# A causal convolution and two MLPs on one core: the startup re-ordered, and the low halves of two chunks made by one subtraction

## The chip, the cores and the metric

The kernel runs on one core of a Trainium2 chip. Its time is the device time of one execution in microseconds, from the first to the last instruction with what lies around it. Three runs of the kernel before took 2321.36, 2321.87 and 2329.53 us; the median is 2321.87 us. The profile comes from a further execution.

## The reference

The input is 4 sequences of 4096 positions with 192 channels. A causal convolution of width 7 (softmax weights, one set per group of 24 channels) is followed by two MLPs of width 2048 on the 16384 positions. The weights of the MLPs arrive in float64.

```python
x_pad = np.concatenate([np.zeros((B, pad, D), dtype=np.float32), x], axis=1)
out = np.einsum('hk,bskhg->bshg', w, x_unf)          # w = softmax(weight), 7 taps
x = out.reshape(B * S, D)
h = x @ w_in;  x = (h - np.tanh(h)) @ w_out          # first MLP
h = np.maximum(x @ moe2_w_in, 0.0);  out = h * h @ moe2_w_out   # second MLP
```

## The kernel before

The positions are cut into 32 blocks of 512. Activations are held with channels on partitions, and each fp32 operand of an MLP product is held as a high and a low part (`h` and `l` at the end of a tile's name); a product is three matmuls, high by high, low by high and high by low. A **unit** (m, b, p) is MLP m, block b and a pair p of two chunks of 128 hidden features, so a block has 8 units in each MLP and the program has 512. The contraction is split into row halves of 64 partitions, so that one matmul of each half can run beside the other on the array.

One step of the main loop (line 554 on) issues, for unit u, the 18 half-height matmuls of its first product (`ph`), and the second product (`pA`, `pB`) of the units two and three steps back. Both are laid into 19 slots of two matmuls. Each chunk of the unit then passes through `act` (line 401) and `split` (line 414). For the first MLP, ScalarE (ACT) makes the tanh, VectorE (DVE) subtracts it from `ph` in place (line 406), ACT casts the high part `gh` (line 417), and DVE subtracts it to give the low part `gl` (line 419). The first chunk of a unit is split at the end of its step. The second is split in the middle of the next step.

All other work is put between these by hand. `side` is a list of operations for each half step, filled by `spread` (line 480): the weights' decoding from float64 bits (`decode_ops`, lines 124 to 160: one ACT operation and four DVE operations on `da`, then casts and subtractions into `wIh`, `wIl`, `wO`), the convolution of later blocks (`tap`, lines 230 and 233), the split of its result into `z` (lines 297 to 303) and the ends of blocks. Every engine takes its instructions in the order in which they are issued. Blocks 0 and 1 run side by side, so that each decoded pair of weights serves two units; `SKEW` (line 454) is how many units of block 0 come ahead of the first of block 1, and with it stand the steps in which the pairs are due (`due`, line 492).

The prologue (line 495) loads, computes the taps, and makes the convolution of blocks 0 and 1. For the channels 128 to 191 of both blocks (`xTb`) and for block 1 (`xTa`), TensorE does it with seven matmuls each against diagonal matrices that ACT writes into a `y` buffer (lines 248 and 254). For block 0's first 128 channels DVE does seven taps. The first pair of weights is decoded in the prologue; the others are spread over the steps.

Of the kernel before, what the change touches and what calls it, by code (L numbers as in the profile page):

```python
# [10 lines left out]
F32 = mybir.dt.float32  # L11
F32R = mybir.dt.float32r
# [3 lines left out]
ALU = mybir.AluOpType  # L16
# [14 lines left out]
def conv_mlp_mlp_kernel(ctx: ExitStack, tc: tile.TileContext, x, weight, w_in1, w_out1, w_in2, w_out2, out):  # L31
# [34 lines left out]
    cv = ctx.enter_context(tc.tile_pool(name="cv", bufs=2))  # L66
    zp = ctx.enter_context(tc.tile_pool(name="zp", bufs=2))
    yp = ctx.enter_context(tc.tile_pool(name="yp", bufs=3))
    work = ctx.enter_context(tc.tile_pool(name="work", bufs=3))
    op = ctx.enter_context(tc.tile_pool(name="op", bufs=1))  # L70
    ps_h = ctx.enter_context(tc.tile_pool(name="ps_h", bufs=4, space=PSUM))
    ps_a = ctx.enter_context(tc.tile_pool(name="ps_a", bufs=2, space=PSUM))
# [17 lines left out]
    def load_w(m, p, parts="io"):  # L90
        if (m, p) not in staged:
            staged[m, p] = dec.tile([P, CW], I64, name="st")
        st = staged[m, p]
        c = 2 * p * P
        if "i" in parts:
            load_in(m, st, c)
        if "o" in parts:
            nc.sync.dma_start(
                out=st[:, CI:].rearrange("p (u d) -> p u d", u=2),
                in_=w_out[m][c : c + 2 * P, :].rearrange("(u p) d -> p u d", u=2),  # L100
            )
# [108 lines left out]

    def load_a(b, q=None):
        if b == 1:
            t = work.tile([P, T], F32, name="t").rearrange("p (a c) -> p a c", c=32)
        else:
            t = cv.tile([P, TH, 32], F32, name="xa", bufs=1)
        xs["A", b] = t
        for j in range(4):
            (q or nc.sync).dma_start(out=t[32 * j : 32 * j + 32], in_=x_of(b)[j])
# [6 lines left out]
    def tap(p, b, k):  # L225
        i = "AB".index(p)
        t, w = xT[p, b], taps[:, i, k : k + 1]
        if k == 0:
            acc[p, b] = cv.tile([P, T], F32, name=f"acc{p}", bufs=1)
            nc.vector.tensor_scalar(acc[p, b], t[:, 0:T], w, None, op0=ALU.mult)  # L230
        else:
            a = acc[p, b]
            nc.vector.scalar_tensor_tensor(a, t[:, k : k + T], w, a, op0=ALU.mult, op1=ALU.add)
# [6 lines left out]

    diag = {}

    def make_diag(p):
        t = diag.setdefault("all", yp.tile([P, 4 * T], F32, name="y") if p == "B" else None)
        for k in range(K):
            n = k + K * (p == "A")
            d = diag[p, k] = t[:, n * P : (n + 1) * P]
            nc.scalar.mul(d, ident, taps[:, "AB".index(p), k : k + 1])

    def pe_conv(p, b):  # L250

        a = acc[p, b] = ps_h.tile([P, T], F32, name="ph")
        for k in range(K):
            nc.tensor.matmul(a, diag[p, k], xT[p, b][:, k : k + T], start=k == 0, stop=k == K - 1)  # L254

    def halo(dst, b, src):
        if b % BPB == 0:
# [80 lines left out]
    def products_2(m, b, p, i):  # L338

        if (m, b) not in acc_t:  # L340
            acc_t[m, b] = [ps_a.tile([P, T], F32, name=n) for n in ("pA", "pB")]
        pA, pB = acc_t[m, b]
        r = slice(0, P) if i is None else half(i)
        to_a, to_b = [], []
        for c in range(2):
            gh, gl = (t[r] for t in g_t[m, b, 2 * p + c])
            w = W[m]["O"][r, p, c]
            to_a += [(pA, w[:, 0:P], gh), (pA, w[:, D + DB :], gh), (pA, w[:, 0:P], gl)]
            to_b += [(pB, w[:, P : D + DB], gh), (pB, w[:, P : D + DB], gl)]
        first, last = p == 0 and i != 1, p == NP - 1 and i != 0  # L350
        flags = lambda ms: [(*q, first and k == 0, last and k == len(ms) - 1) for k, q in enumerate(ms)]
        return flags(to_a) + flags(to_b)
# [47 lines left out]

    def act(m, b, f):
        ph = h_t[m, b, f // 2][f % 2]
        t = t_t[m, b, f] = work.tile([P, T], F32, name="t")
        if m == 0:
            nc.scalar.activation(t, ph, AF.Tanh)  # L405
            nc.vector.tensor_tensor(t, ph, t, op=ALU.subtract)  # L406
        else:
            nc.scalar.activation(t, ph, AF.Relu)  # L408
            if b == 1 and f % 2:
                nc.vector.tensor_tensor(t, t, ph, op=ALU.mult)  # L410
            else:
                nc.scalar.activation(t, t, AF.Square)  # L412

    def split(m, b, f):
        t = t_t.pop((m, b, f))
        gh = work.tile([P, T], F32R, name="gh", bufs=6)
        nc.scalar.copy(gh, t)  # L417
        gl = work.tile([P, T], F32R, name="gl", bufs=6)
        nc.vector.tensor_tensor(gl, t, gh.bitcast(F32), op=ALU.subtract)  # L419
        g_t[m, b, f] = gh, gl  # L420

    def finish_ops(m, b):
        pA, pB = acc_t.pop((m, b))
# [27 lines left out]
        ]  # L451


    SKEW = 4

    def two_blocks(m):

# [37 lines left out]
    def prologue():  # L495
        nc.sync.dma_start(out=wt, in_=weight)
        load_b(0)
        load_a(0)
        load_w(0, 0, "i")
        load_a(1)  # L500
        load_w(0, 0, "o")
        load_w(0, 1)
        warm = wpool.tile([P, 1], F32, name="warm")
        nc.gpsimd.memset(warm, 0.0)
        nc.scalar.activation(warm, warm, AF.Tanh)
        make_identity(nc, ident)
        warm_pe(9)
        make_taps()
        head_b(0)
        warm_pe(7)  # L510
        w0 = decode_ops(0, 0, parts=((0, CI), (CI, CW)))
        z0 = split_ops(0)
        make_diag("B")
        pe_conv("B", 0)
        head_a(0)
        make_diag("A")
        tap("A", 0, 0)
        tap("A", 0, 1)
        tap("A", 0, 2)
        head_a(1)  # L520
        pe_conv("A", 1)
        w0[0]()
        for o in w0[1:4]:
            o()
        w0[4]()
        for k in range(3, K):
            tap("A", 0, k)
        w0[6]()
        z0[0]()
        w0[5]()  # L530
        z0[1]()
        z0[2]()
        for o in w0[7:]:
            o()


    after = {}
    spread(split_ops(1), 1, 4)
    for n in range(1, len(pairs)):
        ops = decode_ops(*pairs[n])  # L540
        if n + 1 < len(pairs):
            ops.insert(1, lambda n=n: load_w(*pairs[n + 1]))
        d = 2 * due[n]
        spread(ops, *((d - 2, d) if n < SKEW else (d - 5, d - 1)))
    side[2 * SKEW] += [lambda: load_a(2), lambda: load_b(2)]
    for b in range(2, NBLK):
        s = 2 * at[0, b, 0]
# [65 lines left out]
```

## Time and profile before

| | us |
|---|---|
| median of three runs | 2321.87 |
| profiled execution | 2329.7 |
| its span, first to last instruction | 2327.9 |
| PE, ACT, DVE busy in the span | 2309.2, 1619.3, 1467.7 |

The profiled execution took 2329.7 us, of which 1.8 lie outside the span. The page divides the span into 40 slices of 58 us and gives each engine's busy share in tenths. The first three slices are the prologue and the steps in which weights are decoded; from then on the rows hardly change. The parts that matter are read from views of single stretches: groups of instructions by shape, the instructions of one engine in order of time with what ended each idle time, and the busy time of each engine in a stretch.

### The profile page before, as it was taken

To read this page: it belongs to the slowest core of one execution; us is meant where nothing else is said; L and a number is where in the kernel's file an instruction comes from. 1 tells how busy PE (TensorE), PEld (TensorE's weight loads), DVE (VectorE), ACT (ScalarE), POOL (GpSimd) and SP (SyncE) were. 2 spreads that over 40 slices of the span, in tenths; PEclk is the share of its full clock that TensorE was granted. 3 is DMA by queue.
4 is the path that set the end of the run, shared out by engine and by line. 5 is a ranking of instruction groups with operands and counts; after the bars stand their busy time and mean duration, and the time that the engine had idled before them with its cause. 6 is when DMAs were issued, how large, how long until landed. Compare 5 with 4: busy or idle time off the path is not lost.

```text
span 2327.9 us, 50435 instructions
## 1 busy us (share of the span) xinstructions
PE 2309.2 (99%) x19500; PEld 1892.5 (81%) x19500; DVE 1467.7 (63%) x2299; ACT 1619.3 (70%) x2866; POOL 1.4 (0%) x15
## 2 busy tenths in 40 slices
PE   9999999999999999999999999999999999999999
PEld 6767888888888888888988888888888888888887
DVE  8986666656666555666557665566665666665553
ACT  5577766777666777667777667776677776677766
POOL 0000000000000000000000000000000000000000
PEclk8999999999999999999999999999999999999999
DMA  5230101101111101111001011010111011110000
GB/s 127 68 83 17 26 13 26 22 14 23 22 17 22 26 10 22 17 22 26 15 17 26 13 26 22 11 26 13 26 22 20 16 22 17 22 22 11 16 13 15
DMA packets 216864, 57.78 MB, mean 25 GB/s; under 512 B 204336, under 2 KB 210480, under 8 KB 216624
## 3 DMA queue, kind: packets, MB, share of 16 engines
q1 hardware_dynamic: 216624, 54.56, 11.6%
q8 instruction: 154, 2.52, 0.5%
q14 instruction: 86, 0.70, 0.1%
HBM read 25.17 MB, written 12.58 MB: 16 GB/s over the span
## 4 chain that ended last, share of the span: by engine, by line
PE 95%; DVE 2%; ACT 1%; issue 1%; DMA 0%; SPq 0%; POOL 0%; DVEq 0%; ACTq 0%; POOLq 0%
PE ph L359 38%; PE pA L359 33%; PE pB L359 22%; PE ph L254 1%; DVE t L406 0%; DVE da L138 0%; ACT gh L417 0%; DVE da L134 0%; PE ph L239 0%; DVE gl L419 0%; ACT t L405 0%; ACT da L124 0%; DVE da L129 0%; DVE wIl L155 0%; ACT t L408 0%
## 5 line engine op out<-in xcount | busy, mean ns | idle before, releaser
L359 PE MATMUL pA<-gh,wO 64*128 64x512 f32 x4088 | 1279.3, 392 | 0.0
L419 DVE TENSOR_TENSOR gl<-t,gh 128x512 fp32r<-128x512 f32 x1024 | 683.4, 688 | 623.2 <-ACT gh L417 589.9
L359 PE MATMUL ph<-z,wIh 64*128 64x512 f32 x3072 | 1011.0, 394 | 9.8 <-DVE t L406 7.4
L359 PE MATMUL ph<-y,wIh 64*128 64x512 f32 x3072 | 1003.2, 391 | 1.9 <-DVE t L410 1.9
L359 PEld LDWEIGHTS pA<-gh,wO 64*128 64x128 f32 x4088 | 753.9, 185 | 86.3 <-ACT gh L417 0.8
L359 PE MATMUL pB<-gl,wO 64*128 64x512 f32 x2044 | 804.4, 394 | 0.0
L359 PE MATMUL pB<-gh,wO 64*128 64x512 f32 x2044 | 801.7, 392 | 0.0
L359 PE MATMUL pA<-gl,wO 64*128 64x512 f32 x2044 | 800.8, 392 | 0.0
L417 ACT CAST gh<-t 128x512 fp32r<-128x512 f32 x1024 | 604.7, 613 | 99.1 <-DVE t L406 94.8
L359 PEld LDWEIGHTS ph<-z,wIh 64*128 64x128 f32 x3072 | 569.0, 185 | 75.3 <-DVE t L406 10.6
L359 PEld LDWEIGHTS ph<-y,wIh 64*128 64x128 f32 x3072 | 566.2, 184 | 60.5 <-DVE t L410 2.7
L359 PE MATMUL ph<-z,wIl 64*128 64x512 f32 x1536 | 604.7, 394 | 0.4 <-DVE wIl L155 0.3
L359 PE MATMUL ph<-y,wIl 64*128 64x512 f32 x1536 | 601.4, 392 | 0.0
L405 ACT ACTIVATE t<-ph 128x512 f32<-128x512 f32 x512 | 305.7, 598 | 364.2 <-PE ph L359 265.0
L406 DVE TENSOR_TENSOR t<-ph,t 128x512 f32<-128x512 f32 x512 | 351.9, 687 | 204.6 <-ACT t L405 203.7
L359 PEld LDWEIGHTS pA<-gl,wO 64*128 64x128 f32 x2044 | 376.8, 184 | 49.3 <-DVE gl L419 0.4
L359 PEld LDWEIGHTS pB<-gh,wO 64*128 64x128 f32 x2044 | 376.8, 184 | 48.0
L359 PEld LDWEIGHTS pB<-gl,wO 64*128 64x128 f32 x2044 | 376.4, 184 | 46.1
L408 ACT ACTIVATE t<-ph 128x512 f32<-128x512 f32 x512 | 305.1, 596 | 153.3 <-PE ph L359 130.4
L412 ACT ACTIVATE t<-t 128x512 f32<-128x512 f32 x504 | 318.8, 633 | 16.0
L359 PEld LDWEIGHTS ph<-z,wIl 64*128 64x128 f32 x1536 | 284.6, 185 | 28.4 <-DVE wIl L155 1.5
L359 PEld LDWEIGHTS ph<-y,wIl 64*128 64x128 f32 x1536 | 282.8, 184 | 27.5
(71 smaller groups left out, 712.0 us busy)
## 6 DMA issues: line engine op xcount, KB each, us to landing
z<-z SPq DMA_DIRECT2D x32, 256.0 KB
y<-y SPq DMA_DIRECT2D x32, 256.0 KB
out<-ua SPq DMA_DIRECT2D x128, 64.0 KB
xa<-in_x SPq DMA_DIRECT2D x124, 64.0 KB
st<-in_moe_w_out SPq DMA_DIRECT2D x16, 384.0 KB
xb<-in_x SPq DMA_DIRECT2D x64, 64.0 KB
st<-in_moe_w_in SPq DMA_DIRECT2D x16, 256.0 KB
out<-tu SPq DMA_DIRECT2D x64, 64.0 KB
```

The costliest lines, as they stand in the source:

```text
L254: nc.tensor.matmul(a, diag[p, k], xT[p, b][:, k : k + T], start=k == 0, stop=k == K - 1)
L359: ins = nc.tensor.matmul(o, w, r, start=start, stop=stop).ins
L405: nc.scalar.activation(t, ph, AF.Tanh)
L406: nc.vector.tensor_tensor(t, ph, t, op=ALU.subtract)
L408: nc.scalar.activation(t, ph, AF.Relu)
L412: nc.scalar.activation(t, t, AF.Square)
L417: nc.scalar.copy(gh, t)
L419: nc.vector.tensor_tensor(gl, t, gh.bitcast(F32), op=ALU.subtract)
```

## The change

There are five edits.

1. `split` makes `gh` and `gl` as tiles of two chunks. Each chunk's cast is made where it was, but the low part of both chunks is made by one subtraction over 1024 columns, behind the cast of the second chunk.
2. The convolution of block 0's first 128 channels is divided: DVE does taps 0 to 4, TensorE taps 5 and 6 into a `pA` bank, and DVE adds the two. ACT makes the diagonals for taps 0 to 4 later.
3. TensorE's convolution of block 1 is issued behind step 0, and the split of its result moves from steps 0 and 1 to steps 1 and 2. The results lie in `pA` and `pB` banks.
4. The second pair of weights is loaded ahead of block 1's input and decoded in the prologue.
5. `SKEW` is 3 instead of 4, which moves the due steps of pairs 3 to 7 back by one. The pool `work` holds two tiles of two chunks of `t` instead of three of one.

```diff
-    def make_diag(p):
+    def make_diag(p, ks=range(K)):
...
-        a = acc[p, b] = ps_h.tile([P, T], F32, name="ph")
-        for k in range(K):
-            nc.tensor.matmul(a, diag[p, k], xT[p, b][:, k : k + T], start=k == 0, stop=k == K - 1)
+        a = ps_a.tile([P, T], F32, name="p" + p)
+        for k in range(first, K):
+            nc.tensor.matmul(a, diag[p, k], xT[p, b][:, k : k + T], start=k == first, stop=k == K - 1)
+        if first:
+            nc.vector.tensor_tensor(acc[p, b], a, acc[p, b], op=ALU.add)
+        else:
+            acc[p, b] = a
...
     def split(m, b, f):
-        t = t_t.pop((m, b, f))
-        gh = work.tile([P, T], F32R, name="gh", bufs=6)
-        nc.scalar.copy(gh, t)
-        gl = work.tile([P, T], F32R, name="gl", bufs=6)
-        nc.vector.tensor_tensor(gl, t, gh.bitcast(F32), op=ALU.subtract)
-        g_t[m, b, f] = gh, gl
+
+        p = f // 2
+        if f % 2 == 0:
+            g_t[m, b, p] = [work.tile([P, 2, T], F32R, name=n, bufs=3) for n in ("gh", "gl")]
+        gh, gl = g_t[m, b, p]
+        nc.scalar.copy(gh[:, f % 2], t_t[m, b, p][:, f % 2])
+        if f % 2:
+            nc.vector.tensor_tensor(gl, t_t.pop((m, b, p)), gh.bitcast(F32), op=ALU.subtract)
...
-    SKEW = 4
+    SKEW = 3
...
         make_diag("B")
         pe_conv("B", 0)
         head_a(0)
-        make_diag("A")
-        tap("A", 0, 0)
-        tap("A", 0, 1)
-        tap("A", 0, 2)
-        head_a(1)
-        pe_conv("A", 1)
-        w0[0]()
-        for o in w0[1:4]:
+        make_diag("A", range(own, K))
+        for k in range(own):
+            tap("A", 0, k)
+        for o in w0[0:5]:
             o()
-        w0[4]()
-        for k in range(3, K):
-            tap("A", 0, k)
+        make_diag("A", range(own))
         w0[6]()
+        w0[5]()
+        for o in w0[7:10]:
+            o()
+        pe_conv("A", 0, own)
         z0[0]()
-        w0[5]()
         z0[1]()
         z0[2]()
-        for o in w0[7:]:
+        for o in w0[10:]:
             o()
...
-    after = {}
-    spread(split_ops(1), 1, 4)
-    for n in range(1, len(pairs)):
+        head_a(1)
+        w1[0]()
+        for o in w1[1:]:
+            o()
...
+    after = {0: [lambda: pe_conv("A", 1)]}
+    spread(split_ops(1), 3, 6)
+    side[0].append(lambda: load_w(0, 2))
+    for n in range(2, len(pairs)):
```

The first place is DVE where the second chunk of a unit ends, here with the decoding of a pair beside it. `t` is a chunk's activation, `gl` its low part, `da` and `wIl` are a pair of weights under decoding. Before:

```order
L406 TENSOR_TENSOR t<-ph,t 128x512
L419 TENSOR_TENSOR gl<-t,gh 128x512 x2
L134 SCALAR_TENSOR_TENSOR da<-st,da 128x768
L138 SCALAR_TENSOR_TENSOR da<-st,da 128x768
L406 TENSOR_TENSOR t<-ph,t 128x512
L155 TENSOR_TENSOR wIl_83<-da,wIh_82 128x384
```

And now, at the same place:

```order
L414 TENSOR_TENSOR t<-ph,t 128x512
L430 TENSOR_TENSOR gl<-t,gh 128x1024
L134 SCALAR_TENSOR_TENSOR da<-st,da 128x768
L138 SCALAR_TENSOR_TENSOR da<-st,da 128x768
L414 TENSOR_TENSOR t<-ph,t 128x512
L155 TENSOR_TENSOR wIl_83<-da,wIh_82 128x384
```

The two subtractions of one chunk each, of which the first belonged to the chunk that was finished earlier, have become one of both; nothing stands between it and the subtraction that finishes the second chunk.

The second place is the start of TensorE's program: `xTb` and `xTa` are the convolution's inputs, `y` the diagonals. Before, the two convolutions stand ahead of step 0 (its matmuls write `ph`):

```order
L254 MATMUL ph<-xTb,y 128x512 x7
L254 MATMUL ph<-xTa,y 128x512 x7
L359 MATMUL ph<-z,wIh_82 128x512
L359 MATMUL ph<-z,wIl_83 128x512
L359 MATMUL ph<-z,wIh_82 128x512 x2
```

And now (the middle of step 0 is left out):

```order
L256 MATMUL pB<-xTb,y 128x512 x7
L256 MATMUL pA<-xTa,y 128x512 x2
L365 MATMUL ph<-z,wIh_82 128x512
...
L365 MATMUL ph<-z,wIh_82 128x512
L256 MATMUL pA<-xTa,y 128x512 x7
L365 MATMUL ph<-z,wIh_82 128x512
```

Two matmuls for block 0 stand where seven for block 1 stood, and those seven stand between step 0 and step 1.

The third place is ACT's program in the prologue. Line 248 (now 250) writes the diagonals, line 124 begins the decoding of the first pair's input half and then of its output half, line 150 casts. Before:

```order
L248 ACTIVATE y<-ua,taps 128x128 x14
L260 COPY xTa<-xTa 128x6
L124 ACTIVATE da<-st 128x384
L150 CAST wIh_82<-da 128x384
L124 ACTIVATE da<-st 128x384
L297 CAST z<-ph 64x512
```

And now:

```order
L250 ACTIVATE y<-ua,taps 128x128 x9
L124 ACTIVATE da<-st 128x384
L150 CAST wIh_82<-da 128x384
L250 ACTIVATE y<-ua,taps 128x128 x5
L124 ACTIVATE da<-st 128x384
L303 CAST z<-pB 64x512
```

Five of the fourteen diagonals have moved behind the cast of the first weights and ahead of the operation with which the output half's decoding begins.

## Rows read from the trace of the kernel before

**Rows 1.** The page: busy time, DVE's busy tenths by slice.

```profile
PE 2309.2 (99%) x19500; PEld 1892.5 (81%) x19500; DVE 1467.7 (63%) x2299; ACT 1619.3 (70%) x2866; POOL 1.4 (0%) x15
...
DVE  8986666656666555666557665566665666665553
```

**Rows 2.** Busy time by stretch: length, engines (instructions), granted clock, DMA share, GB/s.

```profile
22.00:155.00 133.00, 122.86 (x913) 94.97 (x914) 124.60 (x208) 79.92 (x147) 0.00 (x0) 0.94 0.35 90
155.00:200.00 45.00, 43.14 (x364) 33.65 (x362) 33.56 (x56) 38.26 (x70) 0.00 (x0) 1.00 0.15 42
200.00:2250.00 2050.00, 2050.00 (x17575) 1691.22 (x17575) 1268.65 (x1962) 1435.87 (x2529) 0.60 (x6) 1.00 0.10 20
```

**Rows 3.** ACT in order of time: start, duration; first activations of units 0 and 24.

```profile
25.02 0.60 ACT L405 ACTIVATE t<-ph 128x512 f32<-128x512 f32 x1 [1.67 <-PE ph L359]
...
153.12 0.59 ACT L408 ACTIVATE t<-ph 128x512 f32<-128x512 f32 x1
```

**Rows 4.** Waits of PE, 22 to 200 us: total, times, longest.

```profile
PE ph L359 <- DVE t L406: 7.4, 9, 1.7
```

**Rows 5.** DVE in order of time, the end of one unit and the next's start.

```profile
54.12 0.69 DVE L406 TENSOR_TENSOR t<-ph,t 128x512 f32<-128x512 f32 x1
54.72 1.47 DVE L419 TENSOR_TENSOR gl<-t,gh 128x512 fp32r<-128x512 f32 x2
56.10 0.95 DVE L134 SCALAR_TENSOR_TENSOR da<-st,da 128x768 uint32<-128x768 uint32 x1
57.09 0.96 DVE L138 SCALAR_TENSOR_TENSOR da<-st,da 128x768 uint32<-128x768 uint32 x1
57.96 0.68 DVE L406 TENSOR_TENSOR t<-ph,t 128x512 f32<-128x512 f32 x1
```

**Rows 6.** ACT in the same stretch: the cast of the second chunk.

```profile
54.84 0.62 ACT L417 CAST gh<-t 128x512 fp32r<-128x512 f32 x1 [0.87 <-DVE t L406]
```

**Rows 7.** DVE's groups by shape: busy us, mean ns, idle before.

```profile
L419 DVE TENSOR_TENSOR gl<-t,gh 128x512 fp32r<-128x512 f32 x1024 | 683.4, 688 | 623.2 <-ACT gh L417 589.9 <-PE pB L359 10.6
...
L434 DVE TENSOR_TENSOR y<-pA,y 128x512 fp32r<-128x512 f32 x32 | 21.8, 681 | 0.0
...
L138 DVE SCALAR_TENSOR_TENSOR da<-st,da 128x768 uint32<-128x768 uint32 x15 | 14.4, 958 | 0.5
...
L155 DVE TENSOR_TENSOR wIl<-da,wIh 128x384 fp32r<-128x384 f32 x16 | 8.9, 554 | 1.9 <-ACT wIh L150 1.9
L130 DVE TENSOR_SCALAR da<-da 128x768 uint32<-128x768 uint32 x15 | 8.4, 560 | 0.5
```

**Rows 8.** DVE in the prologue, in order of time.

```profile
12.92 0.71 DVE L265 STREAM_TRANSPOSE xTa<-t 128x512 f32<-128x512 f32 x1 [2.69 <-DMA t<-in_x]
13.56 0.32 DVE L129 TENSOR_SCALAR da<-da 128x384 f32<-128x384 f32 x1
...
14.90 0.56 DVE L138 SCALAR_TENSOR_TENSOR da<-st,da 128x384 uint32<-128x384 uint32 x1
15.37 3.11 DVE L233 SCALAR_TENSOR_TENSOR accA<-xTa,taps,accA 128x512 f32<-128x512 f32 x4
```

**Rows 9.** ACT in the prologue: the diagonals, the start of the decoding.

```profile
7.72 4.20 ACT L248 ACTIVATE y<-ua,taps 128x128 f32<-128x128 f32 x14
...
11.92 0.55 ACT L124 ACTIVATE da<-st 128x384 f32<-128x384 f32 x1
15.49 0.51 ACT L150 CAST wIh<-da 128x384 fp32r<-128x384 f32 x1 [3.02 <-DVE da L138]
```

**Rows 10.** PE in the prologue: block 1's convolution, step 0's first matmul.

```profile
16.17 6.17 PE L254 MATMUL ph<-xTa,y 128*128 128x512 f32 x14
...
22.27 0.49 PE L359 MATMUL ph<-z,wIh 64*128 64x512 f32 x1
```

**Rows 11.** Busy time by stretch, cut where the granted clock changes; columns as in Rows 2.

```profile
10.70:27.76 17.06, 16.16 (x46) 7.93 (x45) 13.51 (x25) 7.95 (x19) 0.00 (x0) 1.00 0.49 136
27.76:41.41 13.65, 12.82 (x38) 9.31 (x39) 13.09 (x23) 6.31 (x11) 0.00 (x0) 0.50 0.49 137
```

More of the change, by code (lines that the diff above doesn't have):

```diff
@@ L68, in conv_mlp_mlp_kernel @@
     yp = ctx.enter_context(tc.tile_pool(name="yp", bufs=3))
-    work = ctx.enter_context(tc.tile_pool(name="work", bufs=3))
+    work = ctx.enter_context(tc.tile_pool(name="work", bufs=2))
     op = ctx.enter_context(tc.tile_pool(name="op", bufs=1))
@@ L212, in load_a @@
         if b == 1:
-            t = work.tile([P, T], F32, name="t").rearrange("p (a c) -> p a c", c=32)
+            t = work.tile([P, 2, T], F32, name="t")[:, 0, :].rearrange("p (a c) -> p a c", c=32)
         else:
@@ L241, in conv_mlp_mlp_kernel @@
     diag = {}
-    def make_diag(p):
-        t = diag.setdefault("all", yp.tile([P, 4 * T], F32, name="y") if p == "B" else None)
-        for k in range(K):
+    def make_diag(p, ks=range(K)):
+        if not diag:
+            diag["all"] = yp.tile([P, 4 * T], F32, name="y")
+        t = diag["all"]
+        for k in ks:
             n = k + K * (p == "A")
@@ L248, in make_diag, with pe_conv @@
             nc.scalar.mul(d, ident, taps[:, "AB".index(p), k : k + 1])
-    def pe_conv(p, b):
-        a = acc[p, b] = ps_h.tile([P, T], F32, name="ph")
-        for k in range(K):
-            nc.tensor.matmul(a, diag[p, k], xT[p, b][:, k : k + T], start=k == 0, stop=k == K - 1)
+    def pe_conv(p, b, first=0):
+        a = ps_a.tile([P, T], F32, name="p" + p)
[5 more added lines that the diff above has]
+            acc[p, b] = a
     def halo(dst, b, src):
@@ L345, in products_2 @@
         for c in range(2):
-            gh, gl = (t[r] for t in g_t[m, b, 2 * p + c])
+            gh, gl = (t[r, c] for t in g_t[m, b, p])
             w = W[m]["O"][r, p, c]
@@ L402, in act @@
         ph = h_t[m, b, f // 2][f % 2]
-        t = t_t[m, b, f] = work.tile([P, T], F32, name="t")
+        if f % 2 == 0:
+            t_t[m, b, f // 2] = work.tile([P, 2, T], F32, name="t")
+        t = t_t[m, b, f // 2][:, f % 2]
         if m == 0:
@@ L414, in split @@
     def split(m, b, f):
[L415 to L420 removed]
+        p = f // 2
+        if f % 2 == 0:
+            g_t[m, b, p] = [work.tile([P, 2, T], F32R, name=n, bufs=3) for n in ("gh", "gl")]
[3 more added lines that the diff above has]
+            nc.vector.tensor_tensor(gl, t_t.pop((m, b, p)), gh.bitcast(F32), op=ALU.subtract)
     def finish_ops(m, b):
@@ L498, in prologue @@
         load_a(0)
-        load_w(0, 0, "i")
+        load_w(0, 0)
+        load_w(0, 1)
         load_a(1)
-        load_w(0, 0, "o")
-        load_w(0, 1)
         warm = wpool.tile([P, 1], F32, name="warm")
@@ L511, in prologue @@
         w0 = decode_ops(0, 0, parts=((0, CI), (CI, CW)))
+        w1 = decode_ops(0, 1)
         z0 = split_ops(0)
+        own = 5
         make_diag("B")
@@ L543, in conv_mlp_mlp_kernel @@
         d = 2 * due[n]
-        spread(ops, *((d - 2, d) if n < SKEW else (d - 5, d - 1)))
+        spread(ops, *((1, 4) if n == 2 else (d - 5, d - 1)))
     side[2 * SKEW] += [lambda: load_a(2), lambda: load_b(2)]
```

## The prediction

> **What bounds the kernel now.** I read the page first, then busy time by stretch, then single engines in order of time where the rows change. On the page PE is busy 99% and DVE only 63%, but DVE's tenths begin with 8986 and settle at 5 or 6 [rows 1]. The stretches say why: from 22 to 155 us DVE is busy 124.60 of 133 us (94%) while PE makes 913 matmuls; from 200 to 2250 us DVE is at 62%, PE at 100% with 17575 matmuls in 2050 us [rows 2]. So there are two kernels in one. Most of it is paced by PE: 38 matmuls a unit give 2050 / (17575 / 38) = 4.43 us a unit. The first 24 units, all of the first MLP, are paced by DVE: their activations start at 25.02 and the 25th unit's at 153.12, which is 128.1 / 24 = 5.34 us a unit [rows 3]. That costs 24 x (5.34 - 4.43) = 21.8 us. PE waits there for the subtraction on line 406 [rows 4], which gives back a `ph` bank. Behind that stretch PE never waits, so what is lost or won there stays to the end, and what changes in the other 488 units hides behind PE.
>
> The change touches the 22 us before the first unit and the 128 us of the first 24. In both, DVE's queue is the place to count. A time in DVE's queue moves the end by the same amount, less what falls into the waits that it already has: 133 - 124.60 = 8.4 us, much of it the short gaps between dependent instructions [rows 2].
>
> **One subtraction for two chunks.** Before, DVE's order at the end of a unit is: the subtraction that finishes the second chunk at 54.12, the low part of the first chunk at 54.72 (it needs nothing new), the low part of the second, and the next work at 56.10 [rows 5]. Between, ACT casts the second chunk: it starts at 54.84, when the subtraction has ended, and ends at 55.46 [rows 6]. So the first chunk's low part lies exactly in the time that ACT needs, and DVE hardly stands still: 56.10 - 54.12 = 1.98 us a unit.
>
> After, the row behind the second chunk's subtraction is the merged one, and that needs the second cast. DVE takes its instructions in order, so it stands from 54.81 until 55.50 (0.69 us), and everything behind it (decoding, taps, the next unit's subtraction, for which PE waits) stands with it. Then comes a two-source subtraction of 1024 columns. No row has that shape. From below it costs more than 0.96 us, the 768-column row; from above not more than two of 0.69, 1.38 us [rows 7]. Between the 384-column row (0.554) and the 768-column row (0.958) a column costs 1.05 ns beside a fixed 0.15 us, so I take 0.958 + 256 x 1.05 ns = 1.23 us. The next instruction starts about 0.09 us before the end (57.09 + 0.96 against 57.96 [rows 5]), so it takes 1.14 us of the queue. A unit's end then takes 54.12 to 55.50 and 1.14: 2.52 us, 0.54 more than before. Over the 24 units that DVE paces: 24 x 0.54 = **+13.0 us**. With 0.96 (0.87 of the queue) a unit loses 0.27 and the sum is +6.5; with 1.38 (1.29) it loses 0.69 and the sum is +16.6.
>
> The Trainium skill, on the page VectorE: DVE Perf Modes, section "The TRN2 errata — SBUF-src ops pay a fixed extra latency per instruction", says that an instruction pays its fixed latency once however large the tile, so that one large tile is cheaper than two small ones. The rows agree that there is a fixed part (0.15 us of 0.69). By that rule alone the merge saves; it says nothing of a wait ahead of the instruction, and by itself it is the last rival below.
>
> In the other 232 units of the first MLP the same wait lies in DVE's idle time (38% of it [rows 2]), and in the second MLP the cast needs no DVE result except for the odd chunks of block 1. The low part comes later by half a step, but is read two steps on. I cost both at nothing; if that cover failed, PE would wait in each step, and 0.1 us each would be 49 us.
>
> **The prologue.** Four things happen to DVE's queue.
> - The wait of 2.69 us for block 1's input goes [rows 8], since its transpose is put behind the first pair's decoding, some 8 us later. -2.7.
> - Two taps go (four take 3.11, so 1.55) and one addition from PSUM comes, 0.68 like the subtraction from `pA` [rows 7]. -0.9.
> - ACT has nine diagonals instead of fourteen before the first decoding, and five of 0.30 us [rows 9] before the second. The five taps end at about 10.2 (12.92 - 2.69 [rows 8]) + 1.55 = 11.8, the input half is decoded 1.9 us later (13.56 to 15.46 [rows 8]), at 13.7; ACT casts until 14.2, writes five diagonals until 15.7 and makes the output half's first operation (0.55) until 16.2. DVE has one subtraction of 0.55 in that time and stands for 1.45. +1.45. About 0.5 more goes into short waits for casts that had a chunk's subtraction beside them before; this is an estimate.
> - Step 0 needs `z`, which follows the addition: about 19.7 instead of 22.27 [rows 10]. Its 18 half-height matmuls stand one behind the other, 0.233 us each (two at once take 2 x 2050 / 17575 [rows 2]), and end near 24.1. Block 1's convolution then takes its 6.2 us [rows 10], to 30.3, and step 1's first chunk is ready 12 matmuls and an activation later, at 33.7 or so. DVE's own queue, counted on from 16.2: output half 1.9 (18.1), addition and two subtractions for `z` with a cast between (20.3), `wO` and the transpose (21.5), the second pair's four instructions at 0.56 and 0.96 (24.6, [rows 7]) and its three subtractions with a wait for a cast (26.2), unit 0 with its stall and the four instructions of the third pair (3.1 + 0.6 + 2.5): 32.5. It waits for about 1.5.
>
> The sum is -2.7 - 0.9 + 1.45 + 0.5 + 1.5 = -0.2, call it nothing. The 2.6 us that step 0 starts earlier are not a gain by themselves, because PE isn't what is late: the convolution has moved from ahead of step 0 to behind it, and DVE's queue sets the pace.
>
> **Skew and loads.** The same pairs, taps and splits lie ahead of unit 24 before and after, in another order; with the queue full the order moves nothing. The split of block 1 comes later by a step, its copy to the other half too, and step 3 instead of step 4 waits for it; DVE stands at 40 us then and PE is not ahead. The load of pair 2 is issued at about 20 us and needed at 26. I cost these at nothing. The tail isn't touched: the last low part is needed by the last twelve matmuls alone.
>
> **Sum.** 2329.7 + 13.0 - 0.2 = 2342.5 against the profiled execution, which lies 7.8 above the median. The difference put on the median: 2321.87 + 12.8 = **2334.7 us**.
>
> **The rivals.**
> - *The clock falls in the prologue.* From 27.76 to 41.41 the granted clock was 0.50, its lower level of 1.2 GHz, after a stretch of half-height matmuls with a gap [rows 11]. Now PE ends taps 5 and 6 near 18 and idles until 19.7, then runs half-height matmuls until 24. If the clock falls there, the rest of step 0 (14 matmuls) takes 3.3 us more and about half of block 1's convolution another 3.1; step 1 comes up to 6.4 later and DVE, with an empty queue at 32.5, waits for it. With 5 of it: 2339.7. The Trainium skill, TensorE: Matmul & The Clock Gate, "The HAM clock gate", says that activity releases the throttle; the rows agree in that the clock came back. Against it: the convolution is full-height work and may bring the clock back early.
> - *The stall is mostly covered.* If the merged row costs as little as the 768-column row (+6.5) and some 2.5 of the 8.4 us in which DVE is not busy now take up the rest: +4, 2326. For it: ACT chains that DVE waits for may have come in by then. Against it: DVE's gaps in units like that of rows 5 are under 0.1 us.
> - *The merge saves* (the other side). If the merged subtraction is not held up, because it finds the cast done, a unit's end takes 1.98 - 1.38 + 1.14 = 1.74, that is 0.24 less: 24 x 0.24 = 5.8. With the 3.6 of the first two prologue items and no new waits there: -9.4, 2312.5; with the 2.6 us of step 0's earlier start on top, -12, 2310. It decides only where something of at least 0.6 us lies between the second chunk's subtraction and the merged one. Nothing does in the order.
>
> **How the numbers follow.** The forecast has 0.52 and its own range 2328 to 2339 (6.5 to 16.6 us). The clock has 0.20, the covered stall 0.18, the saving 0.10. The range 2317 to 2345 leaves out the better part of the saving and the worst of the clock (the runs before already differ by 8). A difference under 0.5%, 11.6 us, can't be told from none. Slower by more (over 2333.5): 0.65 of the forecast and all of the clock, 0.34 + 0.20 = 0.54. Faster by more (under 2310.3): 0.06, half of the saving's share and a little. Within: 0.40.
>
> **What would show it.** In the profile after, each of the first 24 merged subtractions should have an idle time of about 0.7 us before it, released by the cast, and last 1.2; a unit with decoding should take 0.5 more, and the 25th unit should start at about 166 instead of 153. DVE should have no wait for block 1's input, one of 1.5 for line 124's second half, and one for step 1's first activation. From 200 us on a unit should take 4.43 as before. It is wrong if the 25th unit starts before 160, if the merged rows show no wait, or if the steady units change.

## The result and the profile after

Four runs of each kernel on one chip: the changed kernel took 2343.78 to 2352.81 us, median 2352.42, the kernel before 2321.36 to 2330.15, median 2325.7. The ratio is 1.0106, 95% interval [1.0084, 1.0128]: it is slower, by some 25 us. The forecast was +12.8 and 2334.7, and 2352.4 lies above its range. The executions of one kernel spread over some 9 us, those of the kernel before in three groups near 2321, 2326.5 and 2330 us, so that medians of a few runs mix them; the parts are therefore told apart below by when a unit's first activation starts in the profiled execution, early enough that the groups haven't parted yet.

| first activation of unit (us) | 1 | 4 | 24 | 40 | 511 |
|---|---|---|---|---|---|
| before | 32.18 | 51.60 | 153.12 | 226.17 | 2314.27 |
| after | 39.85 | 59.01 | 170.55 | 249.19 | 2336.78 |
| later by | 7.67 | 7.41 | 17.43 | 23.02 | 22.51 |

So 7.4 us are lost by unit 4, another 10 by unit 24, 5.6 between units 24 and 40, and nothing after that. The page of the changed kernel has PE as busy as before; DVE has 513 instructions less and is idle more:

```profile
PE 2314.3 (98%) x19504; PEld 2032.2 (86%) x19504; DVE 1418.1 (60%) x1786; ACT 1623.0 (69%) x2866; POOL 1.4 (0%) x15
...
L365 PE MATMUL pA<-gh,wO 64*128 64x512 f32 x4088 | 1281.1, 393 | 9.9 <-DVE y L444 9.9
L430 DVE TENSOR_TENSOR gl<-t,gh 128x1024 fp32r<-128x1024 f32 x512 | 627.4, 1225 | 801.3 <-ACT gh L428 682.7
```

The last number of the `pA` row is new: PE has waited 9.9 us for DVE's line 444. The same three stretches as in [rows 2], for the changed kernel (length, busy time and instructions by engine, granted clock, DMA share, GB/s):

```profile
22.00:155.00 133.00, 115.73 (x793) 84.37 (x794) 107.76 (x164) 69.43 (x128) 0.00 (x0) 0.92 0.32 83
155.00:200.00 45.00, 37.81 (x304) 29.04 (x302) 34.36 (x49) 30.99 (x57) 0.00 (x0) 0.97 0.26 68
200.00:2250.00 2050.00, 2050.00 (x17575) 1830.45 (x17575) 1224.06 (x1503) 1443.70 (x2538) 0.61 (x6) 1.00 0.10 19
```

In the first stretch DVE's busy time fell from 124.60 to 107.76 and PE's matmuls from 913 to 793. DVE isn't fuller, it stands more; this is where a busy share misleads. From 155 to 200 PE made 304 matmuls where it made 364. From 200 on the 17575 matmuls are the same to the last one.

The merged subtraction looks as forecast. DVE in order of time, at the place of [rows 5], and ACT's cast there:

```profile
57.08 0.69 DVE L414 TENSOR_TENSOR t<-ph,t 128x512 f32<-128x512 f32 x1
58.45 1.22 DVE L430 TENSOR_TENSOR gl<-t,gh 128x1024 fp32r<-128x1024 f32 x1 [0.69 <-ACT gh L428]
59.59 0.95 DVE L134 SCALAR_TENSOR_TENSOR da<-st,da 128x768 uint32<-128x768 uint32 x1
```

```profile
57.80 0.62 ACT L428 CAST gh<-t 128x512 fp32r<-128x512 f32 x1 [0.74 <-DVE t L414]
```

DVE stands 0.69 us until the cast is done, the row lasts 1.22, and the next starts 2.51 us behind line 414; forecast were 0.69, 1.23 and 2.52.

The prologue does not look as forecast. All idle times of DVE of 0.15 us and more from 9 to 56 us, without the three ahead of merged rows, after and (those not in [rows 8]) before:

```profile
13.42 0.36 DVE L129 TENSOR_SCALAR da<-da 128x384 f32<-128x384 f32 x1 [1.69 <-ACT da L124]
15.94 0.56 DVE L155 TENSOR_TENSOR wIl<-da,wIh 128x384 fp32r<-128x384 f32 x1 [0.58 <-ACT wIh L150]
17.84 0.36 DVE L129 TENSOR_SCALAR da<-da 128x384 f32<-128x384 f32 x1 [1.35 <-ACT da L124]
26.52 0.56 DVE L155 TENSOR_TENSOR wIl<-da,wIh 128x384 fp32r<-128x384 f32 x1 [0.58 <-ACT wIh L150]
30.82 0.56 DVE L129 TENSOR_SCALAR da<-da 128x768 f32<-128x768 f32 x1 [2.60 <-ACT da L124]
40.48 0.69 DVE L414 TENSOR_TENSOR t<-ph,t 128x512 f32<-128x512 f32 x1 [4.14 <-ACT t L413]
42.11 0.63 DVE L160 TENSOR_TENSOR wO<-da,wO 128x256 fp32r<-128x256 f32 x2 [0.47 <-ACT wO L150]
42.91 0.56 DVE L129 TENSOR_SCALAR da<-da 128x768 f32<-128x768 f32 x1 [0.17 <-ACT da L124]
55.22 0.69 DVE L414 TENSOR_TENSOR t<-ph,t 128x512 f32<-128x512 f32 x1 [1.13 <-ACT t L413]
```

```profile
22.57 0.63 DVE L160 TENSOR_TENSOR wO<-da,wO 128x256 fp32r<-128x256 f32 x2 [0.58 <-ACT wO L150]
23.38 0.56 DVE L129 TENSOR_SCALAR da<-da 128x768 f32<-128x768 f32 x1 [0.19 <-ACT da L124]
27.28 0.56 DVE L155 TENSOR_TENSOR wIl<-da,wIh 128x384 fp32r<-128x384 f32 x1 [0.15 <-ACT wIh L150]
42.25 0.69 DVE L406 TENSOR_TENSOR t<-ph,t 128x512 f32<-128x512 f32 x1 [0.49 <-ACT t L405]
```

They add up to 12.7 us after and, with the 2.69 of [rows 8], to 4.1 before. The two largest have their cause on other engines. At 30.82 DVE waits for ACT, and ACT waited for the output half of pair 2's weights; at 40.48 it waits for unit 1's activation, and ACT for PE:

```profile
29.89 0.90 ACT L124 ACTIVATE da<-st 128x768 f32<-128x768 f32 x1 [2.49 <-DMA st<-in_moe_w_out]
39.85 0.60 ACT L413 ACTIVATE t<-ph 128x512 f32<-128x512 f32 x1 [2.96 <-PE ph L365]
```

PE came late because its clock fell. Step 0's first matmul and block 1's convolution, and the stretches of PE's gap and of what follows (the granted clock stands ahead of the last two numbers):

```profile
21.09 0.79 PE L365 MATMUL ph<-z,wIh 64*128 64x512 f32 x1 [4.98 <-ACT z L304]
...
28.26 8.89 PE L256 MATMUL pA<-xTa,y 128*128 128x512 f32 x14
```

```profile
16.10:21.09 4.99, 0.01 (x1) 0.00 (x0) 3.44 (x8) 2.96 (x9) 0.00 (x0) 0.88 0.22 42
21.09:33.54 12.45, 12.45 (x25) 7.21 (x25) 8.45 (x16) 5.21 (x10) 0.00 (x0) 0.50 0.52 148
```

PE idled 4.98 us until `z` was there, and the granted clock was 0.50, the level of 1.2 GHz, up to 33.54. Step 0 took 7.2 us (21.09 to 28.3) and block 1's convolution 8.89 instead of the 6.17 of [rows 10]. Before, the clock fell too, but 8 us later and beside a DVE that was busy 13.09 of those 13.65 us [rows 11].

The loss behind unit 24 is for the most part one wait and what follows it. PE waits twice for DVE's line 444: 5.29 us up to 138.10, ahead of unit 24, and 4.64 us up to 197.86, behind it. The first leaves no trace by unit 24: from unit 16 to unit 24 the changed kernel takes 42.47 us, and 42.89 with SKEW 4 (e3 below), where the wait is gone. The second is in these rows, DVE's and then PE's:

```profile
194.03 0.95 DVE L134 SCALAR_TENSOR_TENSOR da<-st,da 128x768 uint32<-128x768 uint32 x1
195.01 0.96 DVE L138 SCALAR_TENSOR_TENSOR da<-st,da 128x768 uint32<-128x768 uint32 x1
195.89 0.68 DVE L443 TENSOR_TENSOR y<-tu,y 64x512 fp32r<-64x512 f32 x1
196.55 0.56 DVE L155 TENSOR_TENSOR wIl<-da,wIh 128x384 fp32r<-128x384 f32 x1
197.03 0.69 DVE L444 TENSOR_TENSOR y<-pA,y 128x512 fp32r<-128x512 f32 x1
```

```profile
197.86 0.76 PE L365 MATMUL pA<-gh,wO 64*128 64x512 f32 x1 [4.64 <-DVE y L444]
```

Line 444 is the last subtraction that reads a finished block's `pA`. It stands in DVE's queue behind a pair's decoding, and until it is done its bank isn't free: PE stands 4.64 us. With SKEW 3 the unit that needs that bank comes a step earlier than with 4. Near the end of the wait the granted clock fell to 0.50, from 197.39 to 200.80. The stretch from unit 24's first activation to unit 40's, before and then after:

```profile
153.12:226.17 73.05, 71.19 (x604) 56.17 (x603) 49.73 (x81) 59.04 (x107) 0.00 (x0) 1.00 0.13 34
```

```profile
170.55:249.19 78.64, 72.28 (x601) 65.45 (x599) 47.96 (x62) 59.49 (x108) 0.00 (x0) 0.98 0.12 31
```

Of the 5.6 us that it is longer, PE idles 4.5 (6.36 instead of 1.86) and is busy 1.1 longer with about the same matmuls: that is what the clock costs there.

### The profile page after: what moved, and what is told of

It is laid out like the page before. It is cut to its first block, busy times and chain, and to the rows that moved or that the text cites. A ratio compares the mean times of both kernels' runs of the same rounds, so it can differ in the third digit from the quotient of the medians.

```text
span 2350.4 us, 48933 instructions
## 1 busy us (share of the span) xinstructions
PE 2314.3 (98%) x19504; PEld 2032.2 (86%) x19504; DVE 1418.1 (60%) x1786; ACT 1623.0 (69%) x2866; POOL 1.4 (0%) x15
## 3 DMA queue, kind: packets, MB, share of 16 engines
q1 hardware_dynamic: 216624, 54.56, 11.5%
q8 instruction: 154, 2.52, 0.4%
## 4 chain that ended last, share of the span: by engine, by line
PE 93%; DVE 4%; ACT 2%; issue 1%; DMA 1%; SPq 0%; ACTq 0%; DVEq 0%
PE ph L365 37%; PE pA L365 33%; PE pB L365 22%; DVE t L414 1%; ACT gh L428 1%; DVE da L134 0%; DVE da L138 0%; DVE gl L430 0%; PE pA L256 0%; DMA st<-in_moe_w_in 0%; ACT da L124 0%; DVE da L129 0%; DVE accA L233 0%; SPq L218 0%; DVE wIl L155 0%
## 5 line engine op out<-in xcount | busy, mean ns | idle before, releaser
L430 DVE TENSOR_TENSOR gl<-t,gh 128x1024 fp32r<-128x1024 f32 x512 | 627.4, 1225 | 801.3 <-ACT gh L428 682.7
L365 PE MATMUL ph<-z,wIh 64*128 64x512 f32 x3072 | 991.4, 394 | 14.5 <-DVE t L414 5.4
L365 PE MATMUL ph<-y,wIh 64*128 64x512 f32 x3072 | 985.2, 392 | 0.5 <-DVE t L418 0.5
L365 PEld LDWEIGHTS pA<-gh,wO 64*128 64x128 f32 x4088 | 742.2, 185 | 66.2 <-ACT gh L428 6.3
L365 PEld LDWEIGHTS ph<-z,wIh 64*128 64x128 f32 x3072 | 554.9, 185 | 55.4 <-ACT z L304 5.8
L365 PEld LDWEIGHTS ph<-y,wIh 64*128 64x128 f32 x3072 | 553.2, 185 | 36.2 <-DVE t L418 0.9
L414 DVE TENSOR_TENSOR t<-ph,t 128x512 f32<-128x512 f32 x512 | 346.3, 683 | 98.1 <-ACT t L413 94.0
```

Source lines behind the costliest of these rows:

```text
L365: ins = nc.tensor.matmul(o, w, r, start=start, stop=stop).ins
L430: nc.vector.tensor_tensor(gl, t_t.pop((m, b, p)), gh.bitcast(F32), op=ALU.subtract)
```

## The experiments

In short, later than the kernel before by (us, one profiled execution of each), with the ratio of times:

| kernel | unit 1 | unit 24 | unit 40 | ratio, 95% interval |
|---|---|---|---|---|
| after | 7.7 | 17.4 | 23.0 | 1.0106 [1.0084, 1.0128] |
| e1, two subtractions | 5.8 | 5.9 | 9.7 | 1.0037 [1.0021, 1.0053] |
| e2, before + merge alone | 0.5 | 11.2 | 13.8 | 1.0055 [1.0033, 1.0076] |
| e3, SKEW 4 | 8.4 | 16.9 | 19.4 | 1.0071 [1.0046, 1.0096] |
| e4, PE's gap filled | 3.8 | 12.2 | 18.8 | 1.0071 [1.0044, 1.0098] |
| e5, before + SKEW 3 alone | 0.1 | -0.3 | 4.9 | 1.0008 [0.9994, 1.0022] |
| e6, merged row issued later | 6.8 | 15.2 | 16.7 | 1.0055 [1.0035, 1.0074] |
| e7, before + that | 0.8 | 7.1 | 5.7 | 1.0011 [1.0000, 1.0022] |
| e8, e6 + e3 + e4 | 6.4 | 13.2 | 11.6 | 1.0036 [1.0022, 1.0050] |
| e9, e1 + e3 + e4 | 7.8 | 6.4 | 6.3 | 1.0026 [1.0011, 1.0040] |
| e11, e1 + e3 | 8.4 | 6.6 | 6.4 | 1.0032 [1.0020, 1.0044] |
| e12, e1 + e4 | 2.7 | 3.2 | 7.4 | 1.0042 [1.0027, 1.0056] |
| e13, e9, a decoding later | 4.0 | 5.4 | 5.3 | 1.0024 [1.0010, 1.0038] |
| e10, before, a convolution on PE | -0.1 | 10.4 | 10.4 | 1.0044 [1.0028, 1.0061] |

The lowest time of each kernel, less the lowest of the kernel before that ran beside it, agrees with the column of unit 40 to 0.8 us, but for e6, e8 and e12 (1.3 to 1.8): 22.4 after, 10.0 for e1, 13.1 for e2, 18.7 for e3 and e4. Differences under 1 us between two rows say little.

**The merge, taken out (e1) and alone (e2).** e1 is the changed kernel with this in `split`; e2 is the kernel before with edit 1 of the change and the two tiles in the pool of `t` that go with it.

```diff
-        gh, gl = g_t[m, b, p]
-        nc.scalar.copy(gh[:, f % 2], t_t[m, b, p][:, f % 2])
-        if f % 2:
-            nc.vector.tensor_tensor(gl, t_t.pop((m, b, p)), gh.bitcast(F32), op=ALU.subtract)
+        gh, gl = (g[:, f % 2] for g in g_t[m, b, p])
+        t = t_t[m, b, p][:, f % 2]
+        nc.scalar.copy(gh, t)
+        nc.vector.tensor_tensor(gl, t, gh.bitcast(F32), op=ALU.subtract)
```

> The changed kernel with the low parts of a unit made by two subtractions again, each at its chunk's place; the tiles of two chunks, the prologue and the skew stay. Theory (the stall ahead of the merged subtraction costs 0.54 us in each of the 24 units that DVE paces): 13 us less than the changed kernel, so about 2339 against 2352, and the 25th unit starts near 158 instead of 170.5; the idle time of 0.69 us in front of each low part is gone. Rival (the prologue, the clock and the skew make the whole loss, the stall falls into waits that are there anyway): no more than 3 us less, 25th unit after 167.

> The kernel before with edit 1 alone: tiles of two chunks and the merged subtraction. Theory of the stall: 24 x 0.54 = 13 us slower than before, less up to 3 that falls into DVE's existing waits, 25th unit near 164 to 166 instead of 153. Rival (the stall is covered, the other edits make the loss): within 3 us of before. Rival that the merge saves: 5.8 us faster.

Without the merge unit 40 starts 23.02 - 9.71 = 13.3 us earlier; alone it costs 13.8. It is the largest cause, and its size is near the forecast one. Not all of it falls where it was forecast: at unit 24 it is 11.5 (e1) and 11.2 (e2), and the rest comes behind, where PE waits for the later low part (1.06 us at 188.23 in the changed kernel). ACT's first activations of units 24 and 40 in e1:

```profile
159.00 0.59 ACT L416 ACTIVATE t<-ph 128x512 f32<-128x512 f32 x1
...
235.88 0.60 ACT L413 ACTIVATE t<-ph 128x512 f32<-128x512 f32 x1 [0.94 <-PE ph L365]
```

**SKEW, back to 4 (e3) and alone at 3 (e5).** One line each.

```diff
-    SKEW = 3
+    SKEW = 4
```

> The changed kernel with SKEW 4 instead of 3. Theory (with skew 3 block 1 of the second MLP asks for its pA bank a step earlier, while DVE still has to free it with the last subtraction of block 2: PE waits 4.6 us there, once): that wait shrinks to under 1 us and the kernel takes 4 to 5 us less than the changed one. Rival (DVE's lag is the same and PE has only been let run ahead: what it doesn't wait there it waits later): within 1.5 us of the changed kernel.

> The kernel before with edit 5's SKEW 3 alone. Theory of the bank (block 1 of the second MLP asks for its pA bank one step earlier, and DVE frees it by its own place in the queue): PE waits once or twice for the last subtraction of a block near units 27 to 30, and the kernel is 2 to 4 us slower than before at unit 40. Rival (skew only lets PE run ahead, DVE sets the pace): within 1 us at unit 40.

With 4 both waits for line 444 are gone and unit 40 comes 3.6 us earlier, a little less than expected. In the kernel before, 3 brings the same wait (line 434 there) and costs 4.9, more than I expected, all of it between units 24 and 40. PE's row among the waits of e5, from 22 to 240 us (total, times, longest):

```profile
PE pA L359 <- DVE y L434: 9.3, 2, 5.2
```

The longer wait, 5.2 us up to 123.02, leaves no trace at unit 24, which starts 0.3 earlier than before: DVE sets the pace there. The second, 4.1 up to 178.65, does: from unit 24 to unit 40 PE idles 3.0 us more than before and is busy 2.2 longer, with the granted clock at 0.50 from 177.65 to 184.48. e5's lowest time is 4.9 above the lowest of the kernel before beside it (2325.75 and 2320.85); the ratio of all runs doesn't show it.

**PE's gap filled (e4).** Behind taps 5 and 6, five full-height matmuls whose result nobody reads; the output is unchanged.

```diff
         pe_conv("A", 0, own)
+        ph = ps_h.tile([P, T], F32, name="ph")
+        for _ in range(5):
+            nc.tensor.matmul(ph, diag["B", 0], xT["B", 0][:, 0:T], start=True, stop=True)
```

> The changed kernel with five full-height matmuls of 512 columns, whose result nobody reads, in PE's idle 5 us between block 0's two taps and step 0. Theory (that gap lets the granted clock fall to half from 19.9 to 33.5, and step 0 and block 1's convolution take 3.0 and 2.7 us more; DVE stands idle for them at 36 to 40 us): the clock stays up over step 0 and the convolution, step 1's first activation comes 4 to 6 us earlier than 39.85 and the kernel takes 3 to 6 us less. Rival (the loads and DVE's queue are what is late there, not the clock): the clock stays up and the 25th unit still starts within 1.5 us of 170.5.

The clock then stays at full until 37.53 and is low from there to 44.37; DVE's wait for unit 1's activation is 1.08 us instead of 4.14. Unit 1 starts 3.85 earlier than after, just under the 4 to 6 expected, unit 24 5.3, unit 40 4.2. Not all of the 5.3 is the gap's: the first weights landed earlier too, DVE's wait for them being 0.83 instead of 1.69. Behind unit 24 PE's idle time is that of the changed kernel (6.37), but the clock was low for 6.83 us instead of 3.41, and 1.1 us are lost again.

```profile
21.10:28.00 6.90, 6.90 (x26) 4.07 (x25) 5.66 (x11) 1.92 (x4) 0.00 (x0) 1.00 0.74 191
37.50:44.40 6.90, 6.57 (x25) 5.07 (x27) 5.47 (x10) 3.74 (x7) 0.00 (x0) 0.51 0.30 86
```

```profile
36.62 0.69 DVE L414 TENSOR_TENSOR t<-ph,t 128x512 f32<-128x512 f32 x1 [1.08 <-ACT t L413]
```

**The merged row in a better place (e6 and, from the kernel before, e7).** The merged subtraction is issued behind the one that finishes the next unit's first chunk, so that the cast should long be done.

```diff
-        if f % 2:
-            nc.vector.tensor_tensor(gl, t_t.pop((m, b, p)), gh.bitcast(F32), op=ALU.subtract)
+    def low(m, b, p):
+        gh, gl = g_t[m, b, p]
+        nc.vector.tensor_tensor(gl, t_t.pop((m, b, p)), gh.bitcast(F32), op=ALU.subtract)
...
             act(u[0], u[1], 2 * u[2])
+            if i:
+                low(*units[i - 1])
```

> The changed kernel with the merged subtraction kept, but issued after the next unit's first chunk has been subtracted, so that work stands between the second chunk and it. Theory of the stall (only the place of the merged row costs; the row itself saves 1.98 - 1.74 = 0.24 us a unit): the idle time of 0.69 us in front of it is gone, the 25th unit comes 16 to 19 us earlier than 170.5, and the kernel is 15 to 19 us faster than the changed one. Rival (the merged row loses by something else, its later end or the two-chunk tiles): under 10 us, or new waits of PE for the low part.

> The kernel before with the merged subtraction in the later place and nothing else changed. Theory: 24 x 0.24 = 5.8 us faster than before, the 25th unit near 147.5 instead of 153; this is the saving that the merge holds when its wait is covered. Rival (the fixed part of the second instruction was covered by waits before, so nothing is won): within 1.5 us of before.

Both expectations failed: e6 gains 6.3 us at unit 40, not 15 to 19, and e7 is 5.7 later than before, not earlier. The waits of e6 from 22 to 240 us show what took the place of the stall:

```profile
DVE wO L160 <- ACT wO L150: 15.1, 13, 1.9
PE pA L365 <- DVE gl L432: 12.2, 8, 2.6
```

The low part now comes too late for PE 8 times, 12.2 us (4.0 in the changed kernel, by the page's group of `pA` from `gl`), and with the merged row out of its old place, DVE stands at line 160 for ACT's cast of the output weights, 15.1 us; there is one such wait of 0.5 after. The stall went to the next cast in line.

**The parts together (e8, e9, e11, e12, e13).** e8 is e6, e3 and e4 in one; e9 is e1, e3 and e4; e11 is e9 without the fill; e12 is e1 and e4.

> The changed kernel with the three costs taken out together: merged subtraction in the later place, SKEW 4, five unread matmuls in PE's gap before step 0. If the three account for the loss and the rest of the change is worth about nothing: 23.0 less 13.3 (stall), 5.8 (saving), 4.2 (clock) and 3.6 (bank), that is 4 us faster than before at unit 40. If the divided convolution and the early pair are worth something by themselves: 7 us or more faster. If part of the loss is elsewhere: slower than before.

> The changed kernel with two subtractions a unit, SKEW 4 and five unread matmuls in PE's gap before step 0, so that the divided convolution, the later convolution of block 1 and the early second pair are left. If stall (13.3), bank (3.6 to 4.9) and clock (4.2) make the loss of 23.0 us at unit 40 and nothing else does: between -1 and +3 us against before at unit 40. If more is hidden in the prologue: over +5.

> As e9 without the five matmuls. The clock theory: the granted clock falls in PE's gap before step 0, step 1's first activation comes near 38 to 40, and unit 40 is 4 to 6 us later than in before and 3 to 5 later than in e9. Rival (the clock matters only beside the stall): within 1.5 us of e9.

e8 failed by e6's new waits: 14.0 us of DVE at line 160, 15.4 of PE for the low part. e11 gives the sum: from after to e1 13.3 us, from e1 to e11 (SKEW) 3.3, and 6.4 are left, together 23.0. In another order the share of SKEW is smaller, 1.2 from e12 to e9: behind unit 24 SKEW 4 saves 4.3 us there, but it lost 3.2 ahead of it. e9 came out as its second case, e11 as its rival: where the two others are undone, filling the gap gains 0.1, not 3 to 5. In e9 ACT waits 3.51 us for pair 3's weights, since with SKEW 4 two decodings share the same half steps, and unit 0's second activation stands behind that. The clock, kept up in the gap, was also low later, from 36.66 to 50.31. e13 is e9 with

```diff
-        spread(ops, *((1, 4) if n == 2 else (d - 5, d - 1)))
+        spread(ops, *((1, 4) if n == 2 else (3, 6) if n == 3 else (d - 5, d - 1)))
```

> The changed kernel with two subtractions and with five unread full-height matmuls in TensorE's gap, SKEW left at 3. If the three costs add (merge 13.3, clock fall in the gap 5.3 at unit 24, bank wait of SKEW 3 about 3.5 to 4.9 behind it), unit 24 starts 0 to 1.5 us after its start in the kernel before, unit 40 starts 3.5 to 5.5 after, and the execution is about 4 longer than before. If filling the gap is worth something only together with the merged stall, as the run with all three undone suggests (no gain there), unit 24 stays at +5.9 and unit 40 at +9.7, as with two subtractions alone.

> The kernel with all three undone (two subtractions, SKEW 4, filled gap), with the fourth pair's decoding spread over half steps 3 to 5 instead of 1 to 4. Theory: its +6.3 at unit 40 come from ACT standing 3.5 us for the fourth pair's weights ahead of unit 0's second activation, since two decodings share the same half steps; moved, that wait goes, unit 4 starts 0 to 2 us after the kernel before and unit 40 0 to 2 after; the time is 0 to 2 us above before. Rival: the load itself, behind which the fourth pair's tile is late anyway, sets the pace; then unit 3 waits for its weights instead and unit 40 stays at +5 to +6.5.

e12 lies between its two cases: the fill is worth 2.7 us at unit 24 without the merge, 5.3 beside it. The two largest of DVE's waits in e12, 2.60 and 4.14 after:

```profile
29.43 0.56 DVE L129 TENSOR_SCALAR da<-da 128x768 f32<-128x768 f32 x1 [2.00 <-ACT da L124]
35.51 0.69 DVE L414 TENSOR_TENSOR t<-ph,t 128x512 f32<-128x512 f32 x1 [1.08 <-ACT t L413]
```

Its idle times, listed as above, add up to 8.0 us, 3.9 more than before's 4.1. Less the 0.9 of the moved taps that is 3.0, and unit 24 is 3.2 late: here the list of DVE's idle times is the whole account. e13 failed: unit 1 came 3.8 earlier than in e9, unit 40 only 1.0, and its 5.3 is the number of the rival. As the rival has it, PE now waits for pair 3's weights (0.70 and 1.19 us, up to 46.26 and 47.95), but not because of the load: ACT takes them up at 38.30 without a wait. The 3.24 us of DVE at pair 3's decoding went, but waits of 1.08, 1.08 and 0.26 for activations (1.31 and 0.52 in e9) and 0.66 at a cast and at line 129 stand in its list, and the first weights landed later (1.94 of wait, 1.02 in e9). The list is 10.1, by the same account 5.1 more, against 5.4 measured. Pair 2's load can't be asked for sooner: `st` has two buffers, and it waits until pair 0's is read.

**A remedy for the stretch that DVE paces (e10).** The kernel before, with block 2's 14 taps taken from DVE and given to TensorE, the result copied out by ACT.

```diff
+            nc.tensor.matmul(ph, diag[p, k], xT[p, b][:, k : k + T], start=k == 0, stop=k == K - 1)
+        acc[p, b] = cv.tile([P, T], F32, name=f"acc{p}", bufs=1)
+        nc.scalar.copy(acc[p, b], ph)
```

> The kernel before with the convolution of block 2 (and block 3's upper channels) on TensorE, 14 matmuls of 0.86 us against the diagonals that are there already, and one ACT copy each, in place of 14 DVE taps. If DVE's queue paces the first 24 units: 14 taps of 0.66 are 9.3 us, of which PE gives back some, since it has 0.9 us a unit to spare and gets 12 us more: 4 to 9 us faster than before at unit 24 and at the end. Rival (PE's 12 us come on top, or the bank that the convolution takes makes the steps wait): no faster, or slower.

It came out slower, as the rival has it: PE's time comes on top. DVE is relieved (busy 70.80 of the 95 us from 60 to 155, 89.06 before), and unit 8 starts 2.5 us earlier than before. But a convolution holds PE for 8.0 and for 6.3 us, the next unit's matmuls stand behind it, and DVE waits 6.7 and 7.4 us for their activations. PE's rows, then ACT's:

```profile
79.13 7.97 PE L276 MATMUL ph<-xTa,y 128*128 128x512 f32 x14 [2.53 <-DVE t L417]
...
91.66 6.28 PE L276 MATMUL ph<-xTb,y 128*128 128x512 f32 x14
```

```profile
87.14 0.58 ACT L278 COPY accA<-ph 128x512 f32<-128x512 f32 x1 [5.93 <-PE ph L276]
88.10 0.60 ACT L416 ACTIVATE t<-ph 128x512 f32<-128x512 f32 x1 [0.38 <-PE ph L370]
...
97.97 0.59 ACT L278 COPY accB<-ph 128x512 f32<-128x512 f32 x1 [6.54 <-PE ph L276]
98.93 0.60 ACT L416 ACTIVATE t<-ph 128x512 f32<-128x512 f32 x1 [0.37 <-PE ph L370]
```

ACT's copies stand in its queue for the whole convolution too, but they aren't what holds it up: the activation behind each waits once more for PE.

No version here is faster than the kernel before.

## Why the prediction was wrong

The bound was read rightly in the main: the first 24 units are DVE's, most of the rest is PE's, and what is lost in front stays to the end (23.0 at unit 40, 22.5 at the last unit). No unit behind 40 lost anything. But units 24 to 40, where PE was to run on, lost 5.6.

- *One subtraction for two chunks, +13.0.* Right in the mechanism: a 0.69 us wait, a row of 1.225 us on the mean, and 13.3 us in sum (11.4 to 13.8, by which of the other causes are there). That the sum comes so near has some luck in it: 11.5 (e1) and 11.2 (e2) came in the 24 units that were counted, the rest behind them, where nothing was forecast. The rule weighed there, of the Trainium skill's VectorE: DVE Perf Modes, section "The TRN2 errata — SBUF-src ops pay a fixed extra latency per instruction", holds for the row, 1.225 against two of 0.688, and doesn't decide. e6 and e7 show that the saving isn't had by a later place either.
- *The prologue, "-0.2, call it nothing".* Wrong, and the first failing step: 5.9 us at unit 24 (e1). Item by item: the wait for block 1's input went (-2.7), but 1.69 for the first weights came in its place, which I hadn't looked for; the taps gave 0.9; the wait for the output half is 1.35 (forecast 1.45); casts took 0.9 more (forecast 0.5). Pair 2's weights, "issued at about 20 us and needed at 26", were asked for from 21.59 to 22.81, ACT got them at 29.89, and they cost 2.60 (forecast 0). The wait for unit 1, forecast 1.5, was 4.14.
- *That last one is the rival in which the clock falls*, with a chance of 0.20 and a price of 5. It happened, and its condition was written down: PE idles, then half-height matmuls. Its price by the filled gap is 4.2 to 5.3 beside the merge, some 0.9 of it from earlier weights, 2.3 to 2.7 without, and 0.1 with SKEW 4 (e11 to e9). I took it for the less likely case because a convolution follows; the clock came back only at 33.54, past the middle of it.
- *"With the queue full the order moves nothing".* Wrong, and the second failing step: SKEW 3 costs 3.3 to 4.9 us, or 1.2 where SKEW 4 has a loss of its own (e12 to e9). I asked what DVE's queue holds and not what stands in it ahead of the instruction that frees a `pA` bank. PE waited for it 9.9 us, of which the 4.64 behind unit 24 cost time, with 1.1 of a lower clock.
- *What would show it.* The waits ahead of the merged rows, their length, the wait for the output half and the steady 4.43 us came as written. Unit 24 started at 170.55, not 166, and behind it, where I expected PE to run on, 5.6 us more went.

In sum, 13.3 of 23.0 us have the cause that was forecast, and nearly its size; the two parts costed at nothing brought 3.3 (skew) and 6.4 (prologue).

What stays open: the 6.4 us that are left belong to edits 2, 3 and 4, which no run takes apart; that they are DVE's waits in the list is read from the traces alone. A filled gap is worth 2.7 us in one kernel and 5.3 in another: in DVE's lists the wait for unit 1's activation falls by 2.5 and 3.1, the next one for an activation by 0.6 and 1.1, the wait for the first weights by 0.1 and 0.9, that for pair 2's by 0.6 and 0.0, in sum by 3.7 and 5.1; why 3.7 there bring only 2.7 isn't shown. Why these weights land up to 1.2 us apart in kernels that issue them alike no run shows.

## What to carry to other kernels

Before two instructions are merged, look at what the merged one waits for, in a queue that is served in order: here the first of the two was the work that covered the other's wait, and 0.15 us saved cost 0.69. When an edit "only" moves work, list for each bank and buffer the instruction that frees it and what stands ahead of it in its queue, and for each engine the new gaps; costs booked as nothing made up nearly the whole miss. And when an engine's busy share falls and the time grows, add up its idle times with what ended them: in e9, e11, e12 and e13 that list gave the loss at unit 24 to 0.4 us, in e1 to 0.8. Beside the merge it is not the whole account: with the merge's 11.5 it gives 19.2 for the changed kernel, not 17.4.

## What the runs showed of the hardware

- In a gap of 4.98 us on TensorE the granted clock fell to 1.2 GHz and stayed there until 33.54, though from 21.09 on the engine was busy all the time; with five unread full-height matmuls in the gap the clock stayed at 2.4 GHz through step 0 and block 1's convolution, and fell at 37.53 instead.
- Near the end of a wait of 4.64 us for a bank the granted clock fell to 0.50 for 3.41 us, and in e5, in a wait of 4.11, for 6.83 us. Units 24 to 40 took 5.6 and 5.2 us longer than before; 1.1 and 2.2 of that are PE's longer busy time.
- In the stretch in which PE is always busy, kernels with the same matmuls run at either of two paces. From 230 to 1000 us, at a granted clock of 1.00 in both, the profiled kernel before made 6604 matmuls and e1 6632; from unit 48 to the last they take 4.433 and 4.415 us a unit:

```profile
230.00:1000.00 770.00, 770.00 (x6604) 618.20 (x6602) 480.76 (x745) 541.44 (x953) 0.20 (x2) 1.00 0.11 20
```

```profile
230.00:1000.00 770.00, 770.00 (x6632) 708.77 (x6630) 486.39 (x754) 542.55 (x957) 0.20 (x2) 1.00 0.11 21
```

  Over 470 units that is 8.5 us, the distance between the lowest and the highest group of times. An execution can also change its pace on the way: e11 took 4.415 us a unit up to unit 208 and 4.433 from unit 240 on. What chooses the pace no run here shows.
